# A fused attention, expert and mixing kernel: the end of the attention and the first expert's rows in a new order

## The chip, the core and the metric

The kernel runs on one core of one Trainium2 chip. The core has a matrix engine (TensorE, PE in the profile, with its weight loads shown apart as PEld), a vector engine (VectorE, DVE), a scalar engine (ScalarE, ACT), a general engine (GpSimd, POOL) and a queue engine (SyncE, SP) that issues most of the transfers. Each of them works through its own list of instructions in order, and they wait for each other by semaphores. The metric is the device time of one execution in microseconds (us); lower is better.

## What is computed

Three stages follow each other: a block-wise linear attention with decay, a mixture of experts in which each token goes to one expert, and a gated convolution with an output projection. Cut to what matters here:

```python
def reference(q, k, v, lam, ...):          # q, k, v: 2 x 8 heads x 768 x 64
    attn = linear_attention(q, k, v, lam)  # blocks of positions, one carried state per head
    x = attn.transpose(0, 2, 1, 3).reshape(2, 768, 512)
    # experts
    logits = x @ w_gate                    # 8 experts
    local_gate = sigmoid(x @ w_local)
    for b in range(2):
        for s in range(768):
            fresh = argmax(logits[b, s])
            e = fresh if s == 0 or local_gate[b, s] < 0.5 else prev
            prev = e
            p = softmax(logits[b, s])
            out[b, s] = p[e] * (relu(x[b, s] @ w1[e]) @ w2[e])
    # gated mixing
    gate = sigmoid(causal_conv_5_taps(out, conv_w))
    return (gate * (out @ w_val)) @ w_out
```

## The kernel before, in words

**Tiles.** The 1536 tokens are handled in NT = 12 tiles of 128, six for each batch entry; a tile has a number g from 0 to 11. The attention works on one tile after the other. `scores` and `mask` make the masked products of queries and keys, `mix_state` and `mix` sum the tile's output on TensorE in PSUM, `next_state` and `keep_state` carry the state on. `turned` transposes the finished tile into token rows and multiplies it by the gate weights; `logits` and `choice` find the expert of each token; `choice_turned`, `kept`, `ranks` and `ranks_turned` count, by two scans along the tokens, the place of each token in its expert's list; `slots` copies the places out. `token_rows`, `shift`, `exponents`, `denominator` and `softmax` make the row of a token, 512 values and 8 softmax values, and `softmax` ends with a store of the tile's 128 rows to the DRAM tensor `xd` on SyncE's queue. `index_factors` and `indices` turn the places into the list of row numbers of each expert.

**The first expert's rows.** Expert 0 handles up to 256 tokens. Those that lie in tiles 0 to 8 are fetched: `early_fetch` copies the indices known so far and issues two indirect DMAs on GpSimd, 128 rows each, from `xd` into the two halves t = 0 and 1 of the tile `xr`. They read the rows of tiles 0 to 8, so they wait for the store of tile 8. `early_turn` transposes the fetched rows on TensorE and adds them into the two PSUM tiles px0[0] and px0[1], four transposes for each half t; the profile shows each of them as two matmuls of 128 columns. Those of expert 0's tokens that lie in the last three tiles (ge = 9, g0 = 10, g1 = 11) are not fetched but placed: `parts_hi` and `parts_lo` split a tile's rows into a high and a low part (tile `xs`, two buffers), `places` makes a matrix of ones and zeros (`oh`, two buffers) from the tokens' places, and `place` multiplies the two into px0, eight matmuls for a tile, four for its high and four for its low part. When px0 is complete, `early_split` copies it out of PSUM as a high part (ScalarE) and a low part (VectorE) into `xh0`, and the first expert's first product, `up(0, 0)`, begins: 24 matmuls, of which the first 16 read the high part alone and the last 8 the low part. After it `all_indices` needs the index factors of the three last tiles, and then `up(0, 1)` follows.

**Weights.** The experts' weights come in pieces of 128 x 1024 on SyncE's queue into four `wraw` buffers. Each piece is split into a high part by ScalarE (`split_hi`) and a low part by VectorE (`split_lo`), into one of ten `whl` buffers, which the attention's inputs `qk` and the tile `xh0` share. `first_load`, `first_hi` and `first_lo` do this for the first expert; number 4 is the first piece of its second weight matrix. A `wraw` buffer is free for the next load when its low part is made.

**Order.** All of this stands in a block in which the order on TensorE, VectorE, ScalarE, GpSimd and SyncE is the order of the program. The loop over s = 2 to 11 holds one attention tile in several stages of its pipeline (g1 = s - 1, g2 = s - 2, g3 = s - 3). In it `softmax` of tile g3 is called after `kept`; for tile 8 it is called at the end of pass s = 10. Behind the loop, lines 569 to 616 write out the end of the attention by hand. The experts' block (lines 815 on) is ordered by hand as well, apart from GpSimd.

Of the kernel before, what the change touches and what calls it, by code (L numbers as in the profile page):

```python
# [21 lines left out]
P = 128  # L22
NC = S // P
NT = B * NC
# [17 lines left out]
def fused_kernel(ctx, tc, qkv, lam, wgl, w1, w2, wv, cw, wo, out, dbg=None):  # L42
    nc = tc.nc
# [44 lines left out]
    ident = const.tile([P, P], F32, name="ident")  # L88
# [72 lines left out]
    def split_hi(raw, hl=None, cs=slice(0, 1024)):  # L161
        if hl is None:
            hl = whl_p.tile([P, 2, 1024], F32R, name="whl", tag="whl")
        nc.scalar.copy(hl[:, 0, cs], raw[:, cs])  # L164
        return hl

    def split_lo(raw, hl, cs=slice(0, 1024)):
        nc.vector.tensor_tensor(hl[:, 1, cs], raw[:, cs], hl[:, 0, cs].bitcast(F32), op=SUB)  # L168
# [55 lines left out]
    def first_hi(n, cs=slice(0, 1024)):  # L224
        w = (w1_t if n < 4 else w2_t)[0]
        if len(w) == n % 4:
            w.append(split_hi(raw_t[n], None, cs))
        else:
            split_hi(raw_t[n], w[n % 4], cs)

    def first_lo(n, cs=slice(0, 1024)):
        split_lo(raw_t[n], (w1_t if n < 4 else w2_t)[0][n % 4], cs)
# [9 lines left out]
    def queries(g):  # L242
        if g % NC > 0:
            qs_t[g] = qs = at_p.tile([P, HP, P], F32, name="qs", tag="qs")
            nc.vector.tensor_tensor(qs.rearrange("p (a h) i -> p a (h i)", a=2), qk_t[g][:, 0:2, 0:256],
                                    lq.rearrange("p (a h) i -> p a (h i)", a=2), op=MUL)
# [57 lines left out]
    def decay(g):  # L304
        if 0 < g % NC < NC - 1:
            sd_t[g] = sd = at_p.tile([P, HP, D], F32, name="sdec", tag="sdec")
            for hp in range(HP):
                nc.scalar.activation(sd[:, hp, :], state[g][:, hp, :], AF.Copy, scale=lq[:, hp, P - 1:P])  # L308
# [40 lines left out]
    def parts_hi(g):  # L349
        xs_t[g] = xs = at_p.tile([P, 2, DM], F32R, name="xs", tag="xs")  # L350
        nc.scalar.copy(xs[:, 0], xtok_t[g][:, 0:DM])
# [4 lines left out]
    def shift(g):  # L356
        nmx_t[g] = nmx = at_p.tile([P, 1], F32, name="nmx", tag="nmx")
        nc.scalar.mul(nmx, lg_t[g][1][:, 0:1], -1.0)
# [24 lines left out]
    def softmax(g):  # L383
        (ex, den), xtok = ex_t.pop(g), xtok_t[g]
        nc.scalar.activation(xtok[:, DM:XW], ex, AF.Copy, scale=den[:, 1:2])
        nc.sync.dma_start(xd[1 + g * P:1 + (g + 1) * P, :], xtok)
# [27 lines left out]
    def slots(g):  # L414
        pf = pf_t.pop(g)
        nc.scalar.copy(slot[:, g:g + 1], pf[:, 256:257])
        nc.scalar.copy(soall[:, g, :], pf[:, 256:265])

    def index_factors(g):
        late = g >= ET  # L420
        ab_t[g] = index_parts(tc, keep if late else at_p, slot[:, g:g + 1], colv[:, 0:2 * E], tokid[:, g:g + 1],
                              iota128, str(g) if late else "")
# [10 lines left out]
    oh_t, px0 = {}, []  # L433
# [10 lines left out]
                xr[:, t, :], None, xd[0:1 + ET * P, :], bass.IndirectOffsetOnAxis(ap=idx0[:, t:t + 1], axis=0))  # L444
        oh_t["xr"] = xr

    def early_turn(ks):
        xr = oh_t["xr"]
        for k in ks:
            for t in range(2):  # L450
                nc.tensor.matmul(px0[k // 2][:, k % 2, t * P:(t + 1) * P], xr[:, t, k * P:(k + 1) * P], ident,
                                 start=False, stop=False)

    def places(g):
        oh_t[g] = oh = at_p.tile([P, CAP], F32R, name="oh", tag="oh")
        nc.vector.tensor_scalar(oh, iota256, pf_t[g][:, 256:257] if g == NT - 1 else soall[:, g, 0:1], None,
                                op0=ALU.is_equal)

    def place(g, parts=(0, 1)):
        if not px0:  # L460
            px0.extend(ps_s.tile([P, 2, CAP], F32, name=f"px{i}", tag=f"ps{i}") for i in range(2))
        for i in range(2):
            for a in parts:
                for k in (2 * i, 2 * i + 1):
                    nc.tensor.matmul(px0[i][:, k % 2, :], xs_t[g][:, a, k * P:(k + 1) * P], oh_t[g],
                                     start=(g == ET and a == k % 2 == 0), stop=(g == NT - 1 and a == k % 2 == 1))

    def early_split():
        xh0 = whl_p.tile([P, 2, KD, 2, P], F32R, name="xh0", tag="whl")
        xh_t[0] = xh0  # L470
        for i in range(2):
            v = px0[i].rearrange("p k (t n) -> p k t n", t=2)
            hi = xh0[:, 0, 2 * i:2 * i + 2]
            nc.scalar.copy(hi, v)
            nc.vector.tensor_tensor(xh0[:, 1, 2 * i:2 * i + 2], v, hi.bitcast(F32), op=SUB)
# [8 lines left out]
    with tc.manual_schedule(engines=order_a):  # L484
        warm(10)
        scores(0, 0)
        scores(0, 1)
        mask(0)
        powers()
        keys(0)  # L490
        keys_rest(0)
        load_qk(3)
        load_qk(4)
        warm(2)
        scores(1, 0, True)
        scores(1, 1, True)
        mix_state(0)
        mix(0, 0)
        mix(0, 1)
        mixed(0)  # L500
        next_state(0)
        mask(1)
        keep_state(0)
        queries(1)
        keys(1)
        keys_rest(1)
        turned(0)
        scores(2, 0)
        logits(0)
        choice(0)  # L510
        shift(0)
        token_rows(0)
        exponents(0)
        for s in range(2, NT):
            g1, g2, g3 = s - 1, s - 2, s - 3
            last = s == NT - 1
            if s < NT - 3:
                load_qk(s + 3)
            if s in (2, 4, 6, 8):
                first_load((s - 2) // 2)  # L520
            if s in (10, 11):
                first_load(s - 6)
            scores(s, 1)
            mask(s)
            mix_state(g1)
            mix(g1, 0)
            mix(g1, 1)
            choice_turned(g2)
            kept(g2)
            if g3 >= 0 and not last:  # L530
                softmax(g3)
            mixed(g1)
            ranks(g2, lambda: denominator(g2))
            if g3 >= 0:
                indices(g3)
            if last:
                early_fetch()
            next_state(g1)
            decay(g1)
            queries(s)  # L540
            keys(s)
            keys_rest(s)
            keep_state(g1)
            if s >= 5:
                first_lo((s - 5) // 2, HALF[(s - 5) % 2])
            if not last:
                scores(s + 1, 0)
            turned(g1)
            ranks_turned(g2)
            slots(g2)  # L550
            if last:
                parts_hi(g2)
                softmax(g2)
            logits(g1)
            choice(g1)
            if last:
                places(g2)
                parts_lo(g2)
            else:
                index_factors(g2)  # L560
            shift(g1)
            token_rows(g1)
            exponents(g1)
            if s == NT - 2:
                softmax(g2)
            if 3 <= s < 11:
                first_hi((s - 3) // 2, HALF[(s - 3) % 2])

        ge, g0, g1 = NT - 3, NT - 2, NT - 1
        mix_state(g1)  # L570
        choice_turned(g0)
        kept(g0)
        first_load(6)
        first_load(7)
        mix(g1, 0)
        ranks(g0)
        mix(g1, 1)
        mixed(g1)
        parts_hi(g0)
        first_lo(3, HALF[1])  # L580
        place(ge, (0,))
        turned(g1)
        ranks_turned(g0)
        slots(g0)
        parts_lo(g0)
        denominator(g0)
        softmax(g0)
        logits(g1)
        choice(g1)
        token_rows(g1)  # L590
        parts_hi(g1)
        early_turn((0, 1))
        choice_turned(g1)
        kept(g1)
        places(g0)
        shift(g1)
        exponents(g1)
        ranks(g1)
        place(ge, (1,))
        early_turn((2, 3))  # L600
        place(g0, (0,))
        ranks_turned(g1)
        place(g0, (1,))
        places(g1)
        parts_lo(g1)
        place(g1)
        slots(g1)
        early_split()
        denominator(g1)
        for g in (ge, g0, g1):  # L610
            index_factors(g)
        cd = keep.tile([8, 8], F32, name="cd")
        nc.vector.tensor_scalar(cd, ident[0:8, 0:8], c_all[:, TOK - 1:TOK], None, op0=MUL)
        softmax(g1)
        first_hi(4)
        first_lo(4)
    idx = keep.tile([P, 2 * E], I32, name="idx")
    yslot = keep.tile([P, NT], I32, name="yslot")
    yslot0 = keep.tile([P, 2], I32, name="yslot0")
# [569 lines left out]
```

## Time and profile before

| | |
|---|---|
| device time, median of 3 runs (lowest to highest) | 352.93 us (352.75 to 352.94) |
| the profiled execution: device time, and span of its instructions | 352.89 us, 351.1 us |
| PE busy | 337.4 us, 96% of the span |
| DVE busy | 272.1 us, 77% |
| ACT busy | 197.2 us, 56% |
| the stretch of the hand-written end of the attention | about 69 to 88 us |
| the first expert, up to the second one's first product | about 85 to 109 us |

The profiled execution agrees with the median of the runs to 0.04 us. All times in the rows below are us from the start of its span. An engine that is late costs time only if TensorE, which is at work nearly all the time, has to wait for it in the end. Instructions on one engine overlap by a little at their ends, so a row's duration is up to 0.1 us longer than the step to the next row.

### The profile page before, as it was taken

The page shows a single profiled execution, that of the slowest core. Times are in us where ns is not written, and L with a number is a line of the kernel's source. Part 1 is how long each engine was busy: PE and PEld are TensorE (multiplying, and loading weights), DVE is VectorE, ACT ScalarE, POOL GpSimd, SP SyncE. Part 2 cuts the span into 40 slices and gives each one's busy share as a digit, 9 for nine tenths or more (in the row PEclk, how much of TensorE's full clock was granted, in tenths as well). Part 3 has the DMA queues.
Part 4 walks back from the last instruction along what each step waited for, and adds up shares of the span by engine and source line. Part 5 has one row for each costly group of instructions (what it writes and reads, how often), then busy time and mean ns, then how long its engine had stood idle before and what let it go on. Part 6 is the DMA issues. An engine that isn't in the chain of part 4 may idle for free.

```text
span 351.1 us, 7025 instructions
## 1 busy us (share of the span) xinstructions
PE 337.4 (96%) x2686; PEld 298.0 (85%) x2686; DVE 272.1 (77%) x600; ACT 197.2 (56%) x418; POOL 67.7 (19%) x84
## 2 busy tenths in 40 slices
PE   7999999978998999999999999999999999999994
PEld 3888888858987989889899898898988898899984
DVE  6798999955898977696887786867750699977970
ACT  2577677834454774555645746557442666664631
POOL 3000000020535242131320411221140561000000
PEclk9999999989999999999999999999999999999999
DMA  7997973380569689888698787896720452011012
GB/s 257 393 354 279 318 267 94 118 246 4 179 181 322 201 294 357 254 272 289 214 351 273 231 320 258 276 313 217 275 62 30 137 145 81 33 58 62 34 63 91
DMA packets 24819, 72.00 MB, mean 205 GB/s; under 512 B 3398, under 2 KB 6732, under 8 KB 23628
## 3 DMA queue, kind: packets, MB, share of 16 engines
q1 hardware_dynamic: 20020, 59.87, 50.0%
q0 software_dynamic: 2304, 7.42, 7.0%
q10 hardware_dynamic: 2456, 4.20, 3.2%
q8 instruction: 23, 0.38, 0.5%
q14 instruction: 16, 0.13, 0.1%
HBM read 57.79 MB, written 13.68 MB: 204 GB/s over the span
## 4 chain that ended last, share of the span: by engine, by line
PE 83%; DMA 6%; DVE 5%; ACT 2%; issue 1%; POOL 1%; SPq 0%; DVEq 0%; ACTq 0%
PE py L769 22%; PE ph L757 22%; PE po L983 10%; PE pv L957 8%; PE ps L273 3%; PE po L297 3%; PE po L290 3%; PE rt L337 2%; DMA wraw<-in_w_dram 2%; PE rt L335 2%; DMA qk<-in_qkv_dram 2%; DMA xr<-xd,idx 2%; PE st L317 1%; PE px L733 1%; DMA yg<-ys,yslot 1%
## 5 line engine op out<-in xcount | busy, mean ns | idle before, releaser
L168 DVE TENSOR_TENSOR whl<-wraw,whl 128x1024 fp32r<-128x1024 f32 (+1 forms) x68 | 81.8, 1218 | 17.9 <-ACT whl L164 17.8
L769 PE MATMUL py<-whl,hh 128*128 128x512 f32 x384 | 92.7, 396 | 0.0
L757 PE MATMUL ph<-xh,whl 128*128 128x240 f32 x768 | 89.0, 276 | 1.3 <-DVE whl L168 0.8
L757 PEld LDWEIGHTS ph<-xh,whl 128*128 128x128 f32 x768 | 88.0, 190 | 2.6 <-DVE whl L168 1.0
L769 PEld LDWEIGHTS py<-whl,hh 128*128 128x128 f32 x384 | 70.9, 188 | 16.0
L164 ACT CAST whl<-wraw 128x1024 fp32r<-128x1024 f32 (+1 forms) x68 | 66.4, 994 | 9.2 <-DMA wraw<-in_w_dram 6.0
L760 ACT ACTIVATE hh<-ph 128x480 fp32r<-128x480 f32 x32 | 18.3, 572 | 41.0 <-PE ph L757 40.4
L943 DVE SCALAR_TENSOR_TENSOR gt<-yt,cw_sb,gt 128x256 f32<-128x256 f32 x96 | 39.0, 479 | 1.1 <-ACT gt L935 1.1
L957 PE MATMUL pv<-yh,wv_t 128*128 128x256 f32 x288 | 35.6, 283 | 0.0
L957 PEld LDWEIGHTS pv<-yh,wv_t 128*128 128x128 f32 x288 | 35.1, 191 | 0.5 <-ACT yh L920 0.2
L983 PE MATMUL po<-wo_t,gh 128*128 128x512 f32 (+1 forms) x156 | 34.6, 378 | 0.0
L983 PEld LDWEIGHTS po<-wo_t,gh 128*128 128x128 f32 x156 | 27.3, 188 | 5.8 <-DVE gh L973 0.7
L761 DVE SCALAR_TENSOR_TENSOR hh<-ph,hh 128x480 fp32r<-128x480 f32 x32 | 21.0, 655 | 12.6 <-ACT hh L760 12.6
L776 ACT ACTIVATE yo<-py,pe 128x512 f32<-128x512 f32 x16 | 11.1, 694 | 18.4 <-PE py L769 18.4
L713 POOL DMA_INDIRECT xr<-xd,idx x14 | 19.0, 1355 | 12.2 <-PE px L733 6.9
L443 POOL DMA_INDIRECT xr<-xd,idx x2 | 2.9, 1442 | 66.0 <-ACT sdec L308 65.7
L273 PE MATMUL ps<-qk 64*128 64x128 f32 x176 | 15.3, 295 | 0.0
L899 POOL DMA_INDIRECT yg<-ys,yslot x10 | 11.7, 1167 | 16.0 <-DVE yh L922 11.2
L191 POOL TENSOR_TENSOR f64a<-f64a,f64s 128x512 f32<-128x512 f32 (+1 forms) x9 | 11.4, 1272 | 14.8 <-DVE f64s L190 14.8
L280 DVE TENSOR_TENSOR sm<-ps,dm 128x512 f32<-128x512 f32 x22 | 14.1, 682 | 0.2 <-PE ps L273 0.2
L297 PE MATMUL po<-sm,qk 128*64 128x128 f32 x192 | 13.1, 279 | 0.0
L253 ACT ACTIVATE kd<-qk,dm 128x64 f32<-128x64 f32 x50 | 12.9, 333 | 0.0
(175 smaller groups left out, 424.5 us busy)
## 6 DMA issues: line engine op xcount, KB each, us to landing
wraw<-in_w_dram SPq DMA_DIRECT2D x64, 512.0 KB, 5.8
qk<-in_qkv_dram SPq DMA_DIRECT2D x9, 1024.0 KB, 5.8
ys<-yo ACTq DMA_DIRECT2D x16, 256.0 KB, 6.2
xd<-xtok SPq DMA_DIRECT2D x12, 260.0 KB, 2.6
ys<-warm_sb SPq DMA_DIRECT2D x24, 128.0 KB, 5.3
out_dram<-oo SPq DMA_DIRECT2D x11, 256.0 KB, 2.0
qk<-in_qkv_dram SPq DMA_DIRECT2D x5, 512.0 KB, 6.2
wraw<-in_w_val_dram SPq DMA_DIRECT2D x4, 512.0 KB, 5.4
```

The source lines that it names most:

```text
L164: nc.scalar.copy(hl[:, 0, cs], raw[:, cs])
L168: nc.vector.tensor_tensor(hl[:, 1, cs], raw[:, cs], hl[:, 0, cs].bitcast(F32), op=SUB)
L273: nc.tensor.matmul(ps_t[g][hl][:, hp, :], t[r, half, 256 + c0:256 + c0 + P], t[r, half, c0:c0 + P], start=True, stop=True)
L297: nc.tensor.matmul(po_t[g][hl * D:(hl + 1) * D, hp, :], qk_t[g][:, 3, h * D:(h + 1) * D], sm_t[g][:, hl, hp, :], start=(c == 0), stop=(c = ...
L713: nc.gpsimd.indirect_dma_start(xr[:, t, :], None, xd, bass.IndirectOffsetOnAxis(ap=idx[:, 2 * e + t:2 * e + t + 1], axis=0))
L757: nc.tensor.matmul(ph[:, fi, :], w1_t[e][k][:, a, f * P:(f + 1) * P], xh[:, b, k].rearrange("p t n -> p (t n)")[:, 0:C1], start=first, sto ...
L760: nc.scalar.activation(hh[:, 0, :, 0:C1], ph, AF.Relu)
L761: nc.vector.scalar_tensor_tensor(hh[:, 1, :, 0:C1], ph, 0.0, hh[:, 0, :, 0:C1].bitcast(F32), op0=ALU.max, op1=SUB)
L769: nc.tensor.matmul(py, hhs[f // 2][:, a, f % 2, t * P:(t + 1) * P], w2_t[e][f // 2][:, b, (f % 2) * DM:(f % 2 + 1) * DM], start=(n == 0), ...
L943: nc.vector.scalar_tensor_tensor(gt[:, k, :], yt[:, b, k, c0 + j:c0 + j + 256], cw_sb[:, k, j:j + 1], gt[:, k, :], op0=MUL, op1=ADD)
L957: nc.tensor.matmul(pv[:, mi, :], wv_t[:, a, k * DM + m * P:k * DM + (m + 1) * P], yh[:, b, k, :], start=first, stop=last)
L983: nc.tensor.matmul(po, gh[:, a, k, t * P:(t + 1) * P], wo_t[:, b, k * DM + cs.start:k * DM + cs.stop], start=(i == 0), stop=(i == 11))
```

## The change

The same instructions are issued with the same sizes, in another order:

- `softmax` of tile 8 (one ScalarE instruction and the store) is called in pass s = 10 ahead of `queries` and `keys`, not at the end of the pass.
- On TensorE, behind `ranks_turned` of tile 10: the low part of tile 9 is placed first, then `choice_turned` of tile 11, then the whole of tile 10; `early_turn` now takes one fetched half at a time, four transposes each: two of the first half stand ahead of `ranks_turned` of tile 11, its other two and the four of the second half behind it.
- On ScalarE, `parts_hi` of tile 11 comes behind `kept` of tile 11, and `first_hi(4)` behind `exponents`, ahead of `slots` and `early_split`.
- On VectorE, `first_lo(4)` and the index factors of tiles 9 and 10 come ahead of `early_split`; those of tile 11 stay behind it.

```diff
-    def early_turn(ks):
+    def early_turn(t, ks):
         xr = oh_t["xr"]
         for k in ks:
-            for t in range(2):
-                nc.tensor.matmul(px0[k // 2][:, k % 2, t * P:(t + 1) * P], xr[:, t, k * P:(k + 1) * P], ident,
-                                 start=False, stop=False)
+            nc.tensor.matmul(px0[k // 2][:, k % 2, t * P:(t + 1) * P], xr[:, t, k * P:(k + 1) * P], ident,
+                             start=False, stop=False)
...
             next_state(g1)
             decay(g1)
+            if s == NT - 2:
+                softmax(g2)
             queries(s)
             keys(s)
...
             token_rows(g1)
             exponents(g1)
-            if s == NT - 2:
-                softmax(g2)
...
         logits(g1)
         choice(g1)
         token_rows(g1)
-        parts_hi(g1)
-        early_turn((0, 1))
+        place(ge, (1,))
         choice_turned(g1)
         kept(g1)
         places(g0)
+        parts_hi(g1)
         shift(g1)
         exponents(g1)
         ranks(g1)
-        place(ge, (1,))
-        early_turn((2, 3))
-        place(g0, (0,))
+        place(g0)
+        early_turn(0, (0, 1))
         ranks_turned(g1)
-        place(g0, (1,))
+        early_turn(0, (2, 3))
+        early_turn(1, (0, 1, 2, 3))
+        first_hi(4)
         places(g1)
         parts_lo(g1)
         place(g1)
         slots(g1)
+        first_lo(4)
+        index_factors(ge)
+        index_factors(g0)
         early_split()
         denominator(g1)
-        for g in (ge, g0, g1):
-            index_factors(g)
+        index_factors(g1)
         cd = keep.tile([8, 8], F32, name="cd")
         nc.vector.tensor_scalar(cd, ident[0:8, 0:8], c_all[:, TOK - 1:TOK], None, op0=MUL)
         softmax(g1)
-        first_hi(4)
-        first_lo(4)
```

## Rows read from the trace of the kernel before

**Rows 1.** Chain of work that ended last: start us, us, what.
```profile
71.38 5.73 DMA xr<-xd,idx
...
103.21 6.02 DMA wraw<-in_w_dram
```

**Rows 2.** Windows of 1 us: length, PE, PEld, DVE, ACT, POOL busy, PEclk, DMA, GB/s.
```profile
75.00:76.00 1.00, 0.01 (x1) 0.01 (x1) 0.47 (x3) 0.58 (x1) 0.00 (x0) 1.00 0.86 220
...
79.00:80.00 1.00, 1.00 (x6) 0.96 (x5) 0.00 (x0) 0.00 (x0) 0.00 (x0) 0.50 0.00 0
...
82.00:83.00 1.00, 0.49 (x5) 0.47 (x6) 0.67 (x3) 0.00 (x0) 0.00 (x0) 1.00 0.00 0
```

**Rows 3.** Timeline of TensorE: start us, us, line, operation, out<-in, count, idle before, releaser.
```profile
72.03 0.74 PE L465 MATMUL px<-oh,xs 128*128 128x256 f32 x4
...
75.99 0.49 PE L451 MATMUL px<-ident,xr 128*128 128x128 f32 x2 [1.61 <-DMA xr<-xd,idx]
77.15 1.65 PE L451 MATMUL px<-ident,xr 128*128 128x128 f32 x6 [0.67 <-DMA xr<-xd,idx]
...
80.06 1.27 PE L451 MATMUL px<-ident,xr 128*128 128x128 f32 x8
...
82.51 0.18 PE L411 MATMUL pf<-sel_r,wr 8*128 8x9 f16 x1 [0.68 <-DVE wr L407]
...
84.94 2.96 PE L757 MATMUL ph<-xh,whl 128*128 128x240 f32 x24 [0.20 <-ACT xh L474]
...
88.29 0.17 PE L427 MATMUL pidx<-ixab 128*128 128x16 f16 x1 [0.33 <-DVE ixab L1065]
88.31 2.93 PE L757 MATMUL ph<-xh,whl 128*128 128x240 f32 x24
```

**Rows 4.** Timeline of ScalarE, columns as in Rows 3.
```profile
65.92 0.30 ACT L385 ACTIVATE xtok<-ex,den 128x8 f32<-128x8 f32 x1
...
75.11 0.58 ACT L347 COPY xtok<-rt 128x512 f32<-128x512 f32 x1 [0.25 <-DVE fk L375]
80.35 0.62 ACT L351 CAST xs<-xtok 128x512 fp32r<-128x512 f32 x1 [4.66 <-PE px L465]
80.88 0.25 ACT L396 COPY kp<-pf 8x128 f32<-8x128 f32 x1
```

**Rows 5.** Timeline of VectorE, columns as in Rows 3.
```profile
74.99 0.22 DVE L376 SCALAR_TENSOR_TENSOR fk<-iota,mi,fr 128x8 f16<-128x8 f32 x1
...
81.16 0.47 DVE L400 TENSOR_TENSOR_SCAN o_all<-kp,o_all,pf 8x128 f16<-8x128 f32 x1 [5.69 <-ACT kp L396]
...
83.02 0.69 DVE L354 TENSOR_TENSOR xs<-xtok,xs 128x512 fp32r<-128x512 f32 x1
84.92 1.29 DVE L475 TENSOR_TENSOR xh<-px,xh 128x512 fp32r<-128x512 f32 x2 [1.22 <-ACT xh L474]
...
86.39 0.13 DVE L1061 TENSOR_SCALAR ixs<-slot 128x1 int32<-128x1 int32 x1
...
86.96 0.15 DVE L1061 TENSOR_SCALAR ixs<-slot 128x1 int32<-128x1 int32 x1
...
88.28 1.21 DVE L168 TENSOR_TENSOR whl<-wraw,whl 128x1024 fp32r<-128x1024 f32 x1
...
91.89 0.66 DVE L761 SCALAR_TENSOR_TENSOR hh<-ph,hh 128x480 fp32r<-128x480 f32 x1 [0.41 <-ACT hh L760]
```

**Rows 6.** GpSimd's queue at L443 (ns min/median/max, starts), then its timeline.
```profile
L443 POOLq EVENT_SEMAPHORE  x2: 43/5203/10363, 58.1 to 68.5; - x2
...
69.39 1.68 POOL L443 DMA_INDIRECT xr<-xd,idx  x1 [65.67 <-ACT sdec L308]
```

**Rows 7.** Tile 8's store, issued 66.25: KB, us to landing; then all L158 loads.
```profile
xd<-xtok SPq DMA_DIRECT2D x1, 260.0 KB, 2.2
...
DMA to landing us min/median/max: 4.0/5.8/15.5
```

**Rows 8.** TensorE's waits from 90 us on: us in total, times, longest.
```profile
PE ph L757 <- DVE whl L168: 0.8, 1, 0.8
```

## The prediction

> **What bounds the kernel now.** I read four views in this order. The chain of work that ended last shows where time is not matmul work: it leaves TensorE for the first gather's transfer, 5.73 us, and once more for a weight load of 6.02 us that is issued at 103.21 [rows 1]. The timeline of TensorE shows what this costs: before the first transposes of fetched rows it is idle 1.61 us, then 0.67 us more for the second half, and 0.68 us at `ranks_turned` of tile 11 [rows 3]. The windows show a second price: TensorE does nothing from 75 to 76, and by 79 its granted clock is 0.50, the lower of its two levels; six transposes' matmuls take 1.65 us from 77.15, and eight, half of them past the clock's return, take 1.27 us from 80.06 [rows 2, 3]. The other engines' timelines show why nothing useful fills the hole. `choice_turned` of tile 11 stands behind `early_turn` in TensorE's list, so VectorE waits 5.69 us for `kp`; ScalarE waits 4.66 us to split tile 11, since that needs the `xs` buffer which the late second `place` of tile 9 still reads [rows 4, 5]. So the end of the attention hangs on a gather, although the choice of tile 11 is known at 74.99 + 0.22 = 75.21 [rows 5]. From 90 us on TensorE waits for a weight split only once for more than 0.4 us, 0.8 us [rows 8]; a microsecond won at 85 should therefore reach the end.
>
> **Part 1: the store of tile 8.** ScalarE's instruction (0.30 us [rows 4]) moves some 3 us up, from 65.92 to before `keys`, where its denominator is long made and ScalarE has idle time later in the pass. Its store passes SyncE's queue 3 us sooner and so does `first_load(5)` behind it; nothing else waits there. The gather waits on GpSimd for a semaphore that comes at 58.1 + 10.36 = 68.47, which is the store's issue, 66.25, plus its 2.2 us to landing; the gather itself starts at 69.39 [rows 6, 7]. With the store early, the wait ends with the copied indices, so the gather starts between 67.7 and 68.5 (the 0.9 us from semaphore to start either run beforehand or not), and its halves, used at 75.99 and 77.15 before [rows 3], come 0.9 to 1.7 us sooner. I count this as nothing: part 2 shows that TensorE asks for the halves only at 76.9 and about 78. If the store's move did nothing at all, the halves would still be there.
>
> **Part 2: TensorE's order.** At 74.4 TensorE is through with `ranks_turned` of tile 10 (its idle 1.61 us ends at 75.99 [rows 3]). Then, in the new order:
> - The low part of tile 9, four matmuls; four took 0.74 us with their tail, so about 0.5 us in a row [rows 3]. Done by 74.9, its operands have been ready since before 72. This frees the `xs` buffer.
> - `choice_turned` of tile 11 at 75.21. Its copy `kp` on ScalarE cannot start before `token_rows`, 75.11 + 0.58 = 75.69 [rows 4]. Before, `kp` started at 80.88: 5.19 us later.
> - Tile 10, eight matmuls, about 1.0 us, from 75.5 (VectorE's `oh` is made in place, behind the choice) to 76.5, hidden beside the scans. Two transposes of the first half (four matmuls of 0.11 us, half of what they took at the lower clock, 1.65/6 less the tail) end at 76.9.
> - `ranks_turned` needs the two scans and `wr`. From the start of `kp` to it were 82.51 - 80.88 = 1.63 us [rows 3, 4], so it comes at 77.32; TensorE idles 0.4 us.
> - The six other transposes, twelve matmuls of 0.11 us, end at 78.8. The low part of tile 11 was ready 83.71 - 82.51 = 1.20 us after `ranks_turned` [rows 3, 5], thus at 78.52: `place` of tile 11 starts at 78.8 and does not wait.
> - Before, `up(0, 0)` began 84.94 - 83.71 = 1.2 us after the low part was ready and its first matmul ran [rows 3, 5]; two high ones of 0.12 us go first now: 78.8 + 0.2 + 1.2 = 80.2, against 84.94, 4.7 us earlier.
>
> **Part 3: VectorE's order.** Ahead of the low copies of `early_split` it now does `first_lo(4)`, 1.21 us, and two sets of index factors, 86.96 - 86.39 = 0.57 us each [rows 5]. From 78.52 that is 78.52 + 1.21 + 1.14 = 80.87. The high copies are there at 80.2, so the low ones lie 0.7 us late, and end at 80.87 + 1.29 = 82.16. `up(0, 0)` reads them after 16 of its 24 matmuls, 1.9 us after 80.2, thus at 82.1: covered, by a few hundredths at the second copy. If that cover fails, each us of VectorE costs a us. Then come the denominator and the last index factors. Before, the low copies ended at 86.21 and `indices` of the third tile ran at 88.29 [rows 3, 5], 2.08 us with three sets between; with one set it is 2.08 - 1.14 = 0.94 us: 83.10. `up(0, 0)`, 24 matmuls at (88.29 - 0.33 - 84.94)/24, 0.12 us or a little less, is through at 83.0. So `up(0, 1)` starts at 83.12 against 88.31 [rows 3]: 5.19 us earlier. Rows overlap at their ends by up to 0.1 us, which would add some 0.2 us; I leave it to the range.
>
> **Part 4: ScalarE.** `first_hi(4)` runs behind `exponents`, from about 77.1 to 78.2, where ScalarE would wait anyway; it needs a weight piece whose load is issued in pass 10, ahead of tile 8's store, and one of the `whl` buffers that the last `qk` tiles have left by 72. `slots` of tile 11 comes behind it at 78.2, and no one needs it before 80. Price nothing.
>
> **What is late next.** VectorE was idle 0.41 us for `hh` at 91.89 and then worked through to the weight piece that frees the buffer for the load at 103.21 [rows 1, 5]. Now it has 1.21 us and two sets less to do after 83, so it waits for TensorE's `up(0, 1)` and the whole string moves by 5.19 us, with the load at its end. That load took 6.02 us; such loads take 4.0 to 15.5 us with a median of 5.8 [rows 1, 7]. 1.1 us of it can be won at most, since TensorE waits for that piece's two halves 0.8 us [rows 8] and about 0.3 us; a slow one, some 8 us, gives 2 us back. Sum: 352.89 - 5.19 = 347.7, against a median of 352.93 that the profiled execution meets within 0.04.
>
> **The rivals.**
> - *The clock falls again.* Its fall before came with TensorE idle 1.61 and 0.67 us around two matmuls; idle times of 0.68 and 0.2 us after 82 left it at 1.00 [rows 2, 3]. The new order leaves about 0.3, 0.4 and 0.45 us, with work between, so I expect it to stay. If it falls, the half clock lasts as then, some 3.4 us, and doubles about 1.7 us of matmuls: 349.4. The Trainium skill, "TensorE: Matmul & The Clock Gate", section "A second HAM failure mode: psum-queue depth-cycling", speaks for this rival: it says that frequent short idle times between groups of matmuls are enough to make the clock swing. By that rule the time is 349.4; the row of 82 to 83, TensorE busy for 0.49 at full clock, is against it.
> - *The new work ahead of `early_split` holds it up.* If `first_hi(4)` or `first_lo(4)` finds its buffer or its piece not ready, `slots`, both copies and `up(0, 0)` stand behind it. Half of the gain gone means a wait of 2.6 us: 350.3. Against it: both have been ready for 5 us and more.
> - *The gain is given back at the second expert's weights, and more.* Its mechanism is the one load of 6.02 us: issued 5.19 us earlier, at 98.0, among the same other loads and gathers, it must land by 104.0 for the gain to stand. From a duration of 11.2 us on the kernel is slower than before; at the longest seen, 15.5 us, it is 9.5 us late: 357.2. For it: less time for the same bytes. Against: half of the loads take under 5.8 us, and SyncE's queue gets the buffers sooner, too.
> - *The change doesn't do what it says:* TensorE waits for the gather as before. Then it would have to land after 76.9, later than the 75.99 of before; a delay d costs d - 0.9, and 2 us later gives 348.8.
>
> **How the numbers follow.** Forecast 0.78, the clock 0.09, a hold-up 0.05, the gather 0.03, the load 0.03; an effect under 0.2% 0.02. About 0.2% (0.7 us) is what a measurement of this kernel can tell from no change. The range goes from 347.7 less the 1.1 us of a quick load and 0.2 of overlaps, 346.4, to 347.7 plus the 2 us of a slow load or the clock's 1.7, 349.8. Faster 0.94, within 0.2% 0.03, slower 0.03.
>
> **What would show it.** In the changed kernel's profile: `choice_turned` of tile 11 near 75.2, `kp` near 75.7, no wait of TensorE for the gather, its clock 1.00 through 75 to 85, `up(0, 0)` near 80.2, `up(0, 1)` near 83.1, VectorE's `hh` of the second product near 86.7, and the load of 103.21 issued near 98.0. I am wrong if `kp` still comes behind the gather, if the windows of 76 to 84 show the lower clock, if the low copies end well after 82.2, or if the last load lands much more than 6 us after its issue.

## The result and the profile after

The changed kernel takes 347.73 us (median of 4 runs, 347.24 to 348.00) against 352.94 us: a ratio of 0.985, with a 95% interval of 0.982 to 0.988. The profiled execution took 347.62 us with a span of 345.7 us. The forecast was 347.7. One of the 24 executions of the kernel before that stand beside the store, the filled hole and the choice alone took 545.31 us at a granted clock of 0.558 and is in no ratio below.

The timeline of TensorE in the changed kernel (start us, us, line, operation, out<-in, count, idle before and what ended it) shows the new order. The lines that answer to [rows 3] are these:

```profile
74.30 0.73 PE L464 MATMUL px<-oh,xs 128*128 128x256 f32 x4
75.12 0.22 PE L391 MATMUL pf<-ident,fk 128*8 128x128 f16 x1
75.26 0.22 PE L392 MATMUL pf<-ident,fk 128*8 128x128 f16 x1
75.52 1.22 PE L464 MATMUL px<-oh,xs 128*128 128x256 f32 x8
76.58 0.60 PE L450 MATMUL px<-ident,xr 128*128 128x128 f32 x4
77.22 0.18 PE L411 MATMUL pf<-sel_r,wr 8*128 8x9 f16 x1
...
77.35 1.60 PE L450 MATMUL px<-ident,xr 128*128 128x128 f32 x12
78.71 1.19 PE L464 MATMUL px<-oh,xs 128*128 128x256 f32 x8
80.10 2.96 PE L757 MATMUL ph<-xh,whl 128*128 128x240 f32 x24 [0.20 <-ACT xh L473]
82.90 0.23 PE L427 MATMUL pidx<-ixab 128*128 128x16 f16 x3
82.99 2.94 PE L757 MATMUL ph<-xh,whl 128*128 128x240 f32 x24
```

TensorE no longer waits for the gather. `choice_turned` of tile 11 (L391) comes at 75.12, the placing of tile 10 and the transposes follow it, `up(0, 0)` begins at 80.10 (84.94 in [rows 3]) and `up(0, 1)` at 82.99 (88.31). The windows that answer to [rows 2] (length, PE, PEld, DVE, ACT, POOL busy, granted clock, DMA share, GB/s) show TensorE at work and at its upper clock level all through:

```profile
75.00:76.00 1.00, 0.86 (x7) 0.64 (x7) 0.60 (x4) 0.90 (x3) 0.00 (x0) 1.00 0.84 320
...
79.00:80.00 1.00, 0.90 (x8) 0.69 (x6) 0.96 (x5) 0.54 (x2) 0.00 (x0) 1.00 0.00 0
```

The timelines of ScalarE and VectorE show the string that sets the pace, and the work moved into its gaps:

```profile
75.59 0.25 ACT L396 COPY kp<-pf 8x128 f32<-8x128 f32 x1
...
76.75 1.03 ACT L164 CAST whl<-wraw 128x1024 fp32r<-128x1024 f32 x1
```

```profile
78.33 1.22 DVE L168 TENSOR_TENSOR whl<-wraw,whl 128x1024 fp32r<-128x1024 f32 x1
...
80.65 1.28 DVE L474 TENSOR_TENSOR xh<-px,xh 128x512 fp32r<-128x512 f32 x2
...
86.57 0.66 DVE L761 SCALAR_TENSOR_TENSOR hh<-ph,hh 128x480 fp32r<-128x480 f32 x1 [0.58 <-ACT hh L760]
```

`kp` starts at 75.59 against 80.88 [rows 4]; the low copies of `early_split` run from 80.65 to 81.93 without an idle time before them, behind `first_lo(4)` and two sets of index factors; and VectorE waits 0.58 us for `hh` at 86.57, where it waited 0.41 us at 91.89 [rows 5]. In the chain of waits the weight load of [rows 1] is still there, 5.2 us earlier and as long as before:

```profile
98.00 6.09 DMA wraw<-in_w_dram
```

Over the whole span the distance between the two traces goes like this, each number the start of the same TensorE instruction before less after: 4.84 us at `up(0, 0)`, 5.32 at `up(0, 1)`, 5.15 from the second expert to the last, 4.6 from the second gather of the mixing stage to the end of TensorE's work. The last 0.8 us of the 5.4 us between the two spans lie behind the issue of the last result's store (4.34 us to the end of the span before, 3.55 us after), in a part that no edit touches.

### The profile page after: what moved, and what is told of

It is laid out like the page before. It is cut to its first block, busy times and chain, and to the rows that moved or that the text cites. A ratio compares the mean times of both kernels' runs of the same rounds, so it can differ in the third digit from the quotient of the medians.

```text
span 345.7 us, 7024 instructions
## 1 busy us (share of the span) xinstructions
PE 334.5 (97%) x2686; PEld 296.4 (86%) x2686; DVE 272.5 (79%) x600; ACT 197.4 (57%) x418; POOL 66.2 (19%) x84
## 4 chain that ended last, share of the span: by engine, by line
PE 85%; DVE 7%; DMA 4%; ACT 1%; issue 1%; POOL 0%; DVEq 0%; ACTq 0%
PE ph L757 23%; PE py L769 23%; PE po L983 10%; PE pv L957 9%; PE ps L273 4%; PE po L297 3%; PE po L290 3%; PE rt L337 2%; DMA wraw<-in_w_dram 2%; PE rt L335 2%; PE st L317 1%; DMA yg<-ys,yslot 1%; DVE whl L168 1%; DMA lam_sb<-in_lam_dram 1%; PE px L733 1%
## 5 line engine op out<-in xcount | busy, mean ns | idle before, releaser
L713 POOL DMA_INDIRECT xr<-xd,idx x14 | 18.0, 1289 | 12.2 <-PE px L733 6.9
L191 POOL TENSOR_TENSOR f64a<-f64a,f64s 128x512 f32<-128x512 f32 (+1 forms) x9 | 12.4, 1380 | 14.9 <-DMA wraw<-in_w_dram 9.1
L443 POOL DMA_INDIRECT xr<-xd,idx x2 | 2.7, 1334 | 64.5 <-DMA wraw<-in_w_dram 64.2
L920 ACT CAST yh<-pt 128x512 fp32r<-128x512 f32 x12 | 6.6, 588 | 11.7 <-PE pt L909 10.2
```

The costliest lines, as they stand in the source:

```text
L713: nc.gpsimd.indirect_dma_start(xr[:, t, :], None, xd, bass.IndirectOffsetOnAxis(ap=idx[:, 2 * e + t:2 * e + t + 1], axis=0))
```

## The experiments

The runs came in four sets. The kernel before ran in each, with medians from 353.2 to 355.9 us and a scatter of 2 to 5 us, so two kinds of numbers stand with each experiment: the ratio to the kernel before in the same set with its 95% interval, and the times of five events in the profiled execution. The events are `kp` of tile 11, `up(0, 0)`, `up(0, 1)`, and the issue and the landing of the weight load that was issued at 103.21. The profiled executions differ by up to 0.95 us in when the attention gets going; so I shift each trace such that the first placing of tile 9, which no kernel moves, starts at 72.03 as in [rows 3].

| kernel | `kp` | `up(0, 0)` | `up(0, 1)` | load issued | load landed | ratio (interval) |
|---|---|---|---|---|---|---|
| before | 80.88 | 84.94 | 88.31 | 103.21 | 109.23 | 1 |
| changed | 75.59 | 80.10 | 82.99 | 98.00 | 104.09 | 0.985 (0.982 to 0.988) |
| changed, store back | 75.59 | 80.10 | 82.99 | 97.94 | 104.06 | 0.987 (0.984 to 0.990) |
| changed, VectorE back | 75.59 | 80.10 | 83.47 | 98.37 | 103.92 | 0.985 (0.983 to 0.988) |
| changed, choice late | 77.41 | 81.50 | 84.68 | 99.66 | 105.54 | 0.990 (0.987 to 0.992) |
| changed, fill late | 75.59 | 80.55 | 83.74 | 98.81 | 103.95 | 0.988 (0.983 to 0.994) |
| before + store | 79.60 | 83.71 | 87.08 | 101.98 | 107.92 | 0.996 (0.993 to 0.998) |
| before + filled hole | 80.06 | 84.13 | 87.49 | 102.40 | 108.22 | 0.997 (0.995 to 1.000) |
| before + early choice | 75.59 | 83.53 | 86.90 | 101.80 | 107.79 | 0.999 (0.996 to 1.001) |
| before + fill | 78.32 | 82.39 | 85.75 | 100.66 | 106.24 | 0.995 (0.993 to 0.997) |

**The store back.** In the changed kernel tile 8's softmax and store go back to the end of the pass:

```diff
             decay(g1)
-            if s == NT - 2:
-                softmax(g2)
             queries(s)
...
             exponents(g1)
+            if s == NT - 2:
+                softmax(g2)
```

> The changed kernel with tile 8's softmax and store back at the end of the pass; everything else changed. Theory (the order on TensorE and VectorE makes the gain, the store nothing): the two fetched halves land near 76.0 and 77.1 as in the kernel before, TensorE asks for them at 76.6 and 77.9, so 347.7, within 0.4. Rival (the early store is what takes the gather off the path): TensorE waits for the gather again by about 1.5 us, 349.2.

The landing times of the gather (min/median/max of its two halves, us from issue) and TensorE's two runs of transposes:

```profile
DMA to landing us min/median/max: 6.3/6.7/7.0
...
76.74 0.60 PE L450 MATMUL px<-ident,xr 128*128 128x128 f32 x4
...
77.50 1.60 PE L450 MATMUL px<-ident,xr 128*128 128x128 f32 x12
```

The halves land at 76.5 and 77.9 (issued at 69.49 and 71.52), and TensorE asks at 76.74 and, after two more transposes of the first half, near 78. No idle time stands before either row; all events are within 0.06 us of where the changed kernel has them. But the margin is 0.1 to 0.3 us, and the five times were 347.3 to 349.2, so the two ran side by side in another set.

> As e1_store_back, again, beside the changed kernel on the same chip, since the first look had a spread as wide as what is asked. Theory (the store is worth nothing while the fetched halves land before TensorE asks): the same time as the changed kernel within 0.4. Rival (the halves land so close to the asking that they are late in many executions): 0.5 to 1.5 us longer than the changed kernel.

> The changed kernel itself, unaltered, for a comparison on one chip with the three below: 347.7, within 0.5.

The changed kernel had a median of 349.78 us there (348.87 to 350.98, kernel before 355.9), so its own time was missed in that set, though its ratio, 0.983 (0.979 to 0.987), was not. With the store back it was 350.07 us (348.89 to 351.58), ratio 0.983 (0.979 to 0.988), and its `kp`, `up(0, 0)` and `up(0, 1)` agreed again to 0.02 us. The load did not: it landed at 104.61, against 103.94 in the changed kernel beside it, while in the first execution it had landed at 104.06 against 104.09. Whether those 0.7 us come from the store is not shown. The theory holds within what these runs can tell, some 0.4%; a loss of a few tenths of a us in executions whose gather is slow is not excluded.

**The VectorE part back.** `first_hi(4)`, `first_lo(4)` and the two sets of index factors go behind `early_split`:

```diff
-        first_hi(4)
         places(g1)
...
-        first_lo(4)
-        index_factors(ge)
-        index_factors(g0)
         early_split()
         denominator(g1)
-        index_factors(g1)
+        for g in (ge, g0, g1):
+            index_factors(g)
...
         softmax(g1)
+        first_hi(4)
+        first_lo(4)
```

> The changed kernel with first_hi(4), first_lo(4) and the index factors of tiles 9 and 10 back behind early_split; TensorE's order stays changed. Theory (TensorE's order gives most, VectorE's part only shortens what stands between up(0, 0) and up(0, 1)): the low copies end 0.6 us sooner, three sets of index factors follow, up(0, 1) starts near 83.6 instead of 83.0 and VectorE's hh of the second product 0.6 us later: 348.3. Rival (VectorE bounds the whole stretch up to the weight load, so every us moved off it counts): first_lo(4), 1.21 us, and two sets, 1.14 us, come back in full: 350.0.

VectorE's timeline in this kernel (0.18 us later than the changed kernel's by the shift), and the load from the chain of waits:

```profile
83.62 1.20 DVE L168 TENSOR_TENSOR whl<-wraw,whl 128x1024 fp32r<-128x1024 f32 x1
...
87.21 0.66 DVE L760 SCALAR_TENSOR_TENSOR hh<-ph,hh 128x480 fp32r<-128x480 f32 x1 [0.40 <-ACT hh L759]
...
98.55 5.55 DMA wraw<-in_w_dram
```

`first_lo(4)` takes its 1.20 us, and yet VectorE still waits 0.40 us for `hh`: the time ahead of that product is bounded by TensorE. Only `up(0, 1)` moves, by 0.48 us, and the load's issue by 0.37. The theory expected 0.6 us, the rival 2.35: at `up(0, 1)` the part is worth about half a us. The end does not show it. The load then took 5.55 us instead of 6.09 and landed 0.17 us before the changed kernel's, and the median, 347.85 us, is the changed kernel's within the scatter.

**The choice late.** Two transposes of each half go ahead of `choice_turned`:

```diff
         place(ge, (1,))
+        early_turn(0, (0, 1))
+        early_turn(1, (0, 1))
         choice_turned(g1)
...
         place(g0)
-        early_turn(0, (0, 1))
         ranks_turned(g1)
         early_turn(0, (2, 3))
-        early_turn(1, (0, 1, 2, 3))
+        early_turn(1, (2, 3))
```

> The changed kernel, but two transposes of each fetched half stand ahead of choice_turned of tile 11 again. Theory (the chain from choice_turned over kp, the scans and ranks_turned to up(0, 0) sets the end, one to one): the second half lands at 76.3, choice_turned comes at 76.7 instead of 75.1, kp near 77.1 instead of 75.6, up(0, 0) near 81.4, up(0, 1) near 84.5: 349.2. Rival (what counts is that TensorE has work, in whatever order): TensorE works as much, 347.9.

```profile
76.76 0.71 PE L450 MATMUL px<-ident,xr 128*128 128x128 f32 x4 [0.98 <-DMA xr<-xd,idx]
77.40 0.22 PE L391 MATMUL pf<-ident,fk 128*8 128x128 f16 x1
...
79.35 0.18 PE L411 MATMUL pf<-sel_r,wr 8*128 8x9 f16 x1 [0.53 <-DVE wr L407]
```

`choice_turned` now follows the second half, and TensorE waits for the scans although it placed tile 10 meanwhile. By the table `kp` is 1.82 us later, `up(0, 0)` 1.40 and `up(0, 1)` 1.69; the median is 349.61 us, against 347.7 for the changed kernel in its own runs (ratio 0.990 against 0.985), and the forecast was 349.2. The chain over `kp` is the bound.

**The choice early, fill late.** `choice_turned` stays first, but TensorE waits for the second half before it places tile 10:

```diff
         choice_turned(g1)
...
+        early_turn(0, (0, 1))
+        early_turn(1, (0, 1))
         place(g0)
-        early_turn(0, (0, 1))
         ranks_turned(g1)
         early_turn(0, (2, 3))
-        early_turn(1, (0, 1, 2, 3))
+        early_turn(1, (2, 3))
```

> The changed kernel, with choice_turned still first, but two transposes of each fetched half ahead of the placing of tile 10, so that TensorE waits for the second half with that work behind it. Theory (kp is still early, and the idle time eats only what stands between it and the scans' end): the second half lands at 76.3, tile 10 is placed by 77.7, ranks_turned 0.5 us later than now, place of tile 11 hardly later: 348.0. Rival (filling the wait with the placings is itself the gain): as much as was idle before, 1.5 us: 349.2.

```profile
77.33 0.71 PE L450 MATMUL px<-ident,xr 128*128 128x128 f32 x4 [0.40 <-DMA xr<-xd,idx]
77.79 1.20 PE L464 MATMUL px<-oh,xs 128*128 128x256 f32 x8
78.92 0.18 PE L411 MATMUL pf<-sel_r,wr 8*128 8x9 f16 x1
...
82.36 1.28 DVE L474 TENSOR_TENSOR xh<-px,xh 128x512 fp32r<-128x512 f32 x2
...
99.62 5.14 DMA wraw<-in_w_dram
```

(This trace is 0.81 us late by the shift.) The idle time is 0.40 us, and since the placing of tile 10 now ends after the scans, `ranks_turned` comes 0.9 us later than in the changed kernel. `up(0, 0)` is 0.45 us later, `up(0, 1)` 0.75: between the theory's 0.3 and the rival's 1.5, nearer the theory. The further 0.3 us are the cover of the prediction's part 3 failing: VectorE's low copies end 0.9 us later than in the changed kernel, at 82.83 by the shift, and the last index factors stand behind them.

None of this is left behind the second expert's wait for its weights: the load took only 5.14 us and landed at 103.95, against 103.94 in the changed kernel beside it. The median, 351.65 us against 349.78 for the changed kernel in that set, is 1.9 us longer, but its runs lie between 350.3 and 355.2, and the profiled one lost its time in the mixing stage. There TensorE stood idle for 2.4 us up to 279.2 without a releaser that the profile shows, and the granted clock was 0.50 from 278 to 284. That this comes from the edit is not shown; the events are the better measure.

**The parts alone.** Four kernels add one thing each to the kernel before. First the early store:

```diff
             decay(g1)
+            if s == NT - 2:
+                softmax(g2)
             queries(s)
...
             exponents(g1)
-            if s == NT - 2:
-                softmax(g2)
```

> The kernel before with the early store of tile 8 alone. Theory: the gather starts near 67.9, its halves land near 71.4 and 76.3 instead of 75.9 and 77.1; TensorE's order makes it wait for the second half after one transpose, 0.85 us less than before; the clock still falls, since TensorE is idle nearly as long: 352.1 (350.4 if the clock stays). Rival (the store is the main part): 349 or less.

```profile
74.33 0.49 PE L451 MATMUL px<-ident,xr 128*128 128x128 f32 x2
76.65 0.94 PE L451 MATMUL px<-ident,xr 128*128 128x128 f32 x6 [1.83 <-DMA xr<-xd,idx]
```

One transpose of the first half runs at once, then TensorE waits 1.83 us for the second. The halves land near where they were expected, at 71.5 and 76.6, and the lower clock still comes. `up(0, 0)` is 1.23 us earlier, more than the 0.85 expected: 0.53 us are the second half's earlier start, and 0.71 that the six matmuls behind it now run before the clock falls (0.94 us against 1.65 in [rows 3]). 351.10 us against 353.24 (ratio 0.996) fits that. In the old order the store is worth over a us at `up(0, 0)`, in the new one nothing.

Then the hole filled with ten matmuls on zeros (seven ahead of the first transpose, three behind it), which adds work and moves nothing else:

```diff
-    def early_turn(ks):
+    def early_turn(ks, n=0):
...
                                  start=False, stop=False)
+                if n and k == t == 0:
+                    warm(n)
...
-        early_turn((0, 1))
+        warm(7)
+        early_turn((0, 1), 3)
```

> The kernel before with ten matmuls on zeros, written to a bank nobody reads, in TensorE's wait for the gather, so that it is never idle for long there. Added work, no other change. Theory: the granted clock stays at 1.00 through 77 to 81, the chain from 77.15 on runs 1.6 us sooner, up(0, 0) near 83.2 instead of 84.9: 351.2; so about 1.7 of the 5.2 us are the clock's. Rival (the slow stretch was hidden by other waits): 352.9.

A window of 1 us, then rows of TensorE and `kp` on ScalarE:

```profile
79.00:80.00 1.00, 1.00 (x10) 0.89 (x10) 0.00 (x0) 0.00 (x0) 0.00 (x0) 1.00 0.02 8
...
77.58 0.81 PE L483 MATMUL pwarm<-warm_sb 128*128 128x512 f16 x3
78.23 0.83 PE L451 MATMUL px<-ident,xr 128*128 128x128 f32 x6
...
80.55 0.25 ACT L396 COPY kp<-pf 8x128 f32<-8x128 f32 x1
...
82.18 0.18 PE L411 MATMUL pf<-sel_r,wr 8*128 8x9 f16 x1 [0.89 <-DVE wr L407]
```

The clock stays at 1.00, where [rows 2] show 0.50. But `up(0, 0)` comes only 0.81 us earlier, less than half of what I expected. Most of the difference is a later start. The gather's second half landed 0.25 us later than before in that execution, by the shift, and when it landed TensorE still had 0.33 us of the added matmuls to do, so its six matmuls began 0.58 us later. From their start to `kp` it is 2.32 us here (78.23 to 80.55) and 3.73 before (77.15 to 80.88), and from `kp` to `up(0, 0)` it is the same in both, 4.06: the fallen clock costs 1.4 us. The rest is hidden, as the rival had it for all of it: `ranks_turned` waits 0.89 us for `wr` instead of 0.68.

Then the choice alone:

```diff
-        parts_hi(g1)
-        early_turn((0, 1))
         choice_turned(g1)
         kept(g1)
+        parts_hi(g1)
+        early_turn((0, 1))
         places(g0)
```

> The kernel before with choice_turned and kept of tile 11 alone moved ahead of parts_hi and early_turn. Theory: the chain over kp and the scans is done by 77.2, hidden beside the gather, but TensorE still waits for the gather and then has the whole rest to do, partly at the lower clock; its idle 0.7 us before ranks_turned goes and little else: up(0, 0) near 83.8, 351.8. Rival (this move alone is the gain): 348.5 or less.

```profile
75.50 0.22 PE L391 MATMUL pf<-ident,fk 128*8 128x128 f16 x1 [0.75 <-DVE fk L375]
...
77.01 2.30 PE L451 MATMUL px<-ident,xr 128*128 128x128 f32 x8 [1.15 <-DMA xr<-xd,idx]
```

`kp` is as early as in the changed kernel, 75.59, yet `up(0, 0)` gains only 1.41 us, since TensorE waits for the gather and does all the placing afterwards, the first part at the lower clock (eight matmuls in 2.30 us). The ratio, 0.999 (0.996 to 1.001), shows no gain beyond the noise of that set.

Last, the placings alone:

```diff
-        parts_hi(g1)
+        place(ge, (1,))
+        places(g0)
+        place(g0)
+        parts_hi(g1)
         early_turn((0, 1))
         choice_turned(g1)
         kept(g1)
-        places(g0)
...
-        place(ge, (1,))
         early_turn((2, 3))
-        place(g0, (0,))
         ranks_turned(g1)
-        place(g0, (1,))
```

> The kernel before with the placing of tile 9's low part and of all of tile 10 alone moved ahead of early_turn; choice_turned stays behind the gather, store and VectorE as before. Theory: TensorE works through the wait, so its clock stays at 1.00, the xs buffer is free early, and kp comes right behind the transposes, at 78.0 to 78.4 instead of 80.9; up(0, 0) 2.4 to 2.9 us sooner than before and the same at up(0, 1), where VectorE's three sets still stand: 350.0 to 350.5. Rival (without the early choice nothing of this counts): 352.5 or more.

```profile
76.67 1.50 PE L451 MATMUL px<-ident,xr 128*128 128x128 f32 x8
78.10 0.22 PE L391 MATMUL pf<-ident,fk 128*8 128x128 f16 x1
...
80.05 0.18 PE L411 MATMUL pf<-sel_r,wr 8*128 8x9 f16 x1 [0.58 <-DVE wr L407]
```

`up(0, 0)` is 2.55 us and `up(0, 1)` 2.56 us earlier, within the 2.4 to 2.9 expected; the time, 351.67 us against 353.76, is 2.1 us less, some 0.5 us short of that. The granted clock stays at 1.00 from 74 to 82, so this part holds the price of the fallen clock too. It is the largest single part, but the choice still stands behind the gather.

**A step further.** The next bound by the traces is VectorE's string up to the load at 98.0, with 3 us of conversion in it that belongs to the last stage's weights. This kernel does each of these conversions one expert later:

```diff
-                if e == 0 and j == 3:
-                    split64_a(0)
                 if j == 3 and e > 0:
-                    split64_b(e)
+                    split64_b(e - 1)
+                    if e == E - 1:
+                        split64_a(e)
...
-                if e == 0:
-                    split64_b(0)
-                split64_a(e + 1)
+                split64_a(e)
...
                 last_parts(py)
+                split64_b(e)
                 early_answers_turn()
```

> The changed kernel with each conversion of a value or output weight piece one expert later, so that none stands on VectorE in the first expert, and the last one in the last expert. Theory (after the change the next bound is VectorE's string up to the weight load issued at 98.0): 3.0 us of conversion leave the string and the buffer is free for the second expert's weights, TensorE's waits of 0.8 and 0.5 us for them go: 346.4. Rival (the waits move to the next late piece, or the last expert pays for the added conversion): 347.7 or more.

The chain of waits of this kernel in that stretch, then TensorE's wait for the mixing stage's second gather here:

```profile
97.52 0.63 PE px L733 x8
98.16 5.67 PE py L769 x24
103.83 8.23 PE ph L757 x73
...
PE pt L908 <- DMA yg<-ys,yslot: 0.6, 1, 0.6
```

It is TensorE alone: the waits of 0.8 and 0.5 us for the second expert's weights are gone. Behind the place where they were it is 1.78 us ahead of the changed kernel's trace. Its median was 345.72 us, ratio 0.978 (0.976 to 0.981). Beside the changed kernel:

> As e7_split64_late, again, beside the changed kernel on the same chip. Theory: 1.3 us under the changed kernel for the two waits that are gone, up to 2.1 with the shorter wait for the first gather of the mixing stage. Rival (the first look was a quick one): within 0.5 of the changed kernel.

347.78 us against 349.78, ratios to the kernel before 0.978 (0.974 to 0.983) and 0.983 (0.979 to 0.987): it beats both kernels in both sets. Of its 2.0 us, 1.65 are won by the last expert in the two traces, at those two waits. The wait for the gather of the mixing stage is 0.8 us here and 1.5 in the changed kernel beside it. That it is shorter because of the edit was not shown: it was 0.8 us before the change as well.

## Why the prediction was right

**TensorE's order.** Nearly each step came about 0.1 us before its forecast: `choice_turned` 75.12 (75.21), `kp` 75.59 (75.69), the placing of tile 10 from 75.52 (75.5), `ranks_turned` 77.22 (77.32), the placing of tile 11 from 78.71 (78.8), `up(0, 0)` 80.10 (80.2). The idle 0.4 us expected ahead of `ranks_turned` is not there: the transposes before it run from 76.58 to 77.18. The 0.1 us is the overlap of ScalarE's rows that I had left out at `kp`; it went through the chain unchanged. (TensorE's own rows overlap by more than 0.1 us: 1.60 us from 77.35, and the next row starts at 78.71.) The choice-late and early-choice runs show the chain from both sides: delayed by 1.82 us it delays `up(0, 1)` by 1.69, and brought forward alone it gives 1.41 us, since the other work was not yet done.

**VectorE's order.** The low copies started at 80.65 (80.87) and ended at 81.93 (82.16), `indices` were done behind `up(0, 0)` without a wait of their own, and `up(0, 1)` came at 82.99 (83.12). The load was issued at 98.00, as forecast, and took 6.09 us. The 0.48 us of the VectorE-back run is the price of this part at `up(0, 1)`; in the forecast it stood inside the 5.19 us and not by itself.

**The load.** What reaches the end is the landing of this load, not a us at `up(0, 1)` one to one. In twelve traces (the table's ten, and the second ones of the changed kernel and of the store back) the last expert's first product starts 137.56 to 137.58 us after the load has landed, while `up(0, 1)` lies anywhere from 82.99 to 88.31: TensorE waits for that weight piece, 0.6 to 1.0 us at the longest, in all of them. The landing moved from 109.23 to 104.09, by 5.14 us. The prediction had it as a condition, that the load must land by 104.0; it was met to 0.1 us because this load took 6.09 us against 6.02 before. In the other traces it took 5.14 to 6.12 us, so up to about a us won or lost ahead of it can vanish or double.

**The store.** Counted at nothing, and nothing at `up(0, 1)` by its removal. One step of it was off: I expected both halves 0.9 to 1.7 us sooner, 74.3 to 75.1 for the first. It landed at 71.37, 3.5 us after its issue, the second at 76.30. The gather's own start was 67.90, 0.3 us behind the copied indices (67.47 + 0.14 on ScalarE), at the early end of what I gave.

```profile
67.90 1.15 POOL L443 DMA_INDIRECT xr<-xd,idx  x1 [64.18 <-DMA wraw<-in_w_dram]
...
DMA to landing us min/median/max: 3.5/5.2/6.9
```

**The rivals.** In this stretch the clock did not fall in any run that fills the wait, though idle times remained, up to 0.98 us in the choice-late kernel. The clock's swing under short idle times that the Trainium skill reports of another kernel in "TensorE: Matmul & The Clock Gate", section "A second HAM failure mode: psum-queue depth-cycling", did not show here: TensorE was busy 0.86 from 75 to 76 at 1.00. The price of a fall was put a little high: 1.7 us by counting matmuls at half rate, 1.4 us measured in place, since the wait for `wr` hid the rest. `first_hi(4)` met no wait (76.75, right behind `exponents`), and the late load was as long as before.

**The sum.** 5.19 us against 5.21 between the medians, and 5.15 in the traces where the experts run. That the first two agree to 0.02 us is luck: `up(0, 1)` won 5.32, the wait for the second expert's weights grew by 0.17, the one for a gather of the mixing stage from 0.8 to 1.4 us, and 0.8 us came back behind the last store. The last two were not in the forecast and nearly cancel, and both vary whatever the kernel: over all traces that gather's wait is 0.6 to 1.6 us, and the end behind the last store 3.5 to 4.6. The 0.7 us that I gave as what a measurement can tell was too small as well, since the medians of the kernel before lie up to 3 us apart between sets. The range's upper end, 347.7 plus 2, is 349.7 and not 349.8.

**How the parts add.** Alone in the old order, store, choice and fill bring 1.23, 1.41 and 2.56 us at `up(0, 1)`; taken out of the new order, 0.00, 1.69 and 0.75. By the landing of the load they bring 1.31, 1.44 and 2.99 alone; taken out, the choice costs 1.45, the fill nothing, and the store nothing in one trace and 0.7 in the other. The parts partly replace each other: with the wait filled, the gather's time does not matter, and with the choice and the gather early, the fill is worth less than alone.

## What to carry to other kernels

When an engine waits for a transfer in a hand-written order, look for the short steps behind the wait whose inputs are ready and that start a chain on other engines; they go first, long work without followers fills the rest, and the consumer of the transfer goes last. Work out the new order by adding the old distances between the same instructions: offsets such as from `kp` to `ranks_turned`, 1.63 us, were the same in the new one. And measure a part both by adding it to the old kernel and by taking it out of the new one: a part can be worth 1.2 us the first way and nothing the second. Then look for the next point where all kernels wait for the same thing, here one weight load, and read each part's worth there.

## What the runs showed of the hardware that was not expected

A gather of 128 rows of 2080 B took 3.4 to 3.7 us from issue to landing where it was issued at 67.9, ahead of the next store and load (eight traces), and 5.7 to 7.7 us in all the other early gathers, issued 1.5 us later or behind its twin. The same gather in the same place varied by almost a us between executions: its first half landed 6.6 us after issue in the kernel before, 7.0 with the store back, 7.2 with the early choice and 7.4 with the filled hole. On GpSimd, 0.92 us passed between the semaphore of the store and the gather's start where that was the last wait (68.47 to 69.39), and 0.3 us where the index copy was (67.61 to 67.90). That would fit if part of the instruction's preparation ran while it waits for the second one; no run here separates the two.

The weight load that the second expert waits for took 5.14 to 6.12 us in twelve traces, with the same bytes at the same place in the program. What sets its time is not shown.
